# Retention streamed in 128-token tiles of all heads, transposes by DMA, and a different split of ELU over the engines

## The chip, the cores and the metric

The kernel runs on one core of one Trainium2 chip. The metric is the device time of one execution in microseconds (us). Most executions of one kernel agree within about 1%. A run counts as slow when it is over 1.5% above the fastest run of the same kernel. Ratios use the others, the fast runs: a ratio is the mean time of one kernel's fast runs over the mean time of the other's fast runs of the same rounds, so it is not quite the ratio of the medians that are quoted. In brackets stands its 95% interval. Under 1, the new kernel is faster.

Names used below: PE is TensorE (matrix products), ACT is ScalarE, DVE is VectorE, POOL is GpSimd, SP is SyncE (here it only starts DMAs). In these kernels PE writes its products to tiles in PSUM; all other tiles lie in SBUF. FFN is the feed-forward part, FFN1 its first product and FFN2 its second.

## The reference

```python
# B, H, S, D = 8, 8, 576, 64; all inputs and the output are float32
scores = (1 / sqrt(D)) * q @ k.T                    # per batch and head
gamma  = 1 - 2.0 ** (-5 - arange(H))
ret    = scores * (gamma ** (i - j) if i >= j else 0)   # decay, causal, no softmax
x      = (ret @ v)  -> transposed to tokens x (H*D) = (4608, 512)
h      = x @ w_in                                   # 512 x 2048
g      = where(h > 0, h, exp(min(h, 0)) - 1)        # ELU
out    = g @ w_out                                  # 2048 x 512
```

Because the decay is a product of a factor for row i and one for row j, both kernels multiply q and k by it once and only mask the scores. It also means that everything before a block of tokens can be folded into a D x D state per head: `state = sum over earlier tokens of k_j v_j^T`.

Both kernels compute ELU as `min(max(h, 0), exp(h) - 1)`: `exp` on ACT, then a subtraction of 1, then one max/min instruction on DVE. This identity holds as `exp(h) - 1 >= h`.

## The kernel before

It treats one batch at a time. For each pair of heads it forms the lower triangle of the scores over 576 tokens in four 128-blocks and a tail of 64; only between the first 256 tokens and the rest does it use a state. A generator yields pieces of that work, which the program deals out between the FFN pieces; the order on PE is the scheduler's.

```python
    def attn(b, loads):
        ...                                     # (cut: tails)
        def prep(hp):                           # one head pair, 512 tokens
            ...
            nc.vector.tensor_tensor(qn, r["q"]..., gq..., ALU.mult)
            nc.gpsimd.tensor_tensor(kn, r["k"]..., gk..., ALU.mult)
            nc.scalar.copy(vn.transpose([0, 2, 1, 3]), r["v"])
            return qn, kn, vn

        def trans(hp, qn, kn):                  # q, k turned on PE, copied out by ACT
            ...
            for i, n in enumerate((qn, kn)):
                for t in range(2):
                    nc.tensor.transpose(p0[:, i, t * P : (t + 1) * P], n[:, t], ident)
            nc.scalar.copy(qkT[:, :, :C0], p0)
            ...                                 # (cut: the other two blocks and the tail)

        def scores(qkT, blocks, mask):
            n = mask.shape[1]
            sc = [ps_s.tile([P, n], FP32, name="sc", tag="sc") for _ in range(2)]
            for kt, lo, hi in blocks:
                for i in range(2):              # the two heads of the pair
                    r = slice(i * D, (i + 1) * D)
                    nc.tensor.matmul(sc[i][:, o : o + hi - lo],
                        qkT[r, 1, kt * P : (kt + 1) * P], qkT[r, 0, lo:hi], ...)
                ...
            for i in range(2):
                nc.vector.tensor_tensor(p, sc[i], mask, ALU.mult)
        ...
        for hp in range(HP):
            ...
            pa = scores(qkT, ((0, 0, C0), (1, P, C0), (4, FT * P, S)), mask0)
            yield
            pb = scores(qkT, ((2, C0, S), (3, C0 + P, S)), mask1)
            ...                                 # (cut: products with v and the state)

    def ffn1(g, ft):                            # 128 of 2048 columns, 512 tokens
        xt = xt_tile(g)
        ph = ps_h.tile([P, TG], FP32, name="ph", tag="ph")      # 3 buffers
        for j in range(KJ):
            nc.tensor.matmul(ph, w_in_sb[:, j, ft * P : (ft + 1) * P], xt[:, j], ...)
        e = epool.tile([P, TG], FP32, name="e", tag="e")
        nc.scalar.activation(e, ph, AF.Exp)
        nc.gpsimd.tensor_scalar_add(e, e, -1.0)
        gt_ = gpool.tile([P, TG], BF16, name="g", tag="g")
        nc.vector.scalar_tensor_tensor(gt_, ph, 0.0, e, ALU.max, ALU.min)

    for g in range(NTG + 1):                    # 9 groups of 512 tokens
        ...                                     # (cut: loads two batches ahead)
        for s in range(NFT):
            if g < NTG: ffn1(g, s)
            if g > 0:   ffn2(g - 1, s)
            for _ in range(2 if s % 2 == 0 else 1):
                next(steps, None)               # a piece of batch g + 1
```

Of the kernel before, what the change touches and what calls it, by code (L numbers as in the profile page):

```python
# [17 lines left out]
def kernel(  # L18
# [17 lines left out]
    C0 = 256  # L36
    C1 = S - C0
    FT = 4
    ST = S - FT * P
    KJ = DM // P  # L40
# [4 lines left out]
    assert (DM, S, D, ST) == (H * D, 576, 64, 64)  # L45

    const = ctx.enter_context(tc.tile_pool(name="const", bufs=1))
    raw = ctx.enter_context(tc.tile_pool(name="raw", bufs=5))
    nat = ctx.enter_context(tc.tile_pool(name="nat", bufs=4))
    tpool = ctx.enter_context(tc.tile_pool(name="tpool", bufs=3))  # L50
    ppool = ctx.enter_context(tc.tile_pool(name="ppool", bufs=4))
    wst = ctx.enter_context(tc.tile_pool(name="wst", bufs=6))
    xpool = ctx.enter_context(tc.tile_pool(name="xpool", bufs=3))
    gpool = ctx.enter_context(tc.tile_pool(name="gpool", bufs=2 * NFT + 2))
    epool = ctx.enter_context(tc.tile_pool(name="epool", bufs=5))
# [4 lines left out]
    ps_t = ctx.enter_context(tc.tile_pool(name="ps_t", bufs=1, space=PSUM))  # L60
    ps_s = ctx.enter_context(tc.tile_pool(name="ps_s", bufs=2, space=PSUM))
    ps_o = ctx.enter_context(tc.tile_pool(name="ps_o", bufs=1, space=PSUM))


    ident = const.tile([P, P], BF16, name="ident")
    make_identity(nc, ident)

# [3 lines left out]
    for h in range(H):  # L71
        nc.vector.memset(lgt[:, h : h + 1], lg[h])
    pos_i = const.tile([P, FT + 1], I32, name="pos_i")
# [3 lines left out]
    pos = const.tile([P, FT + 1], FP32, name="pos")  # L77
# [8 lines left out]
    expo = const.tile([P, FT + 1, H], FP32, name="expo")  # L86
    nc.vector.tensor_tensor(
        expo,
        pos.unsqueeze(2).to_broadcast([P, FT + 1, H]),
        lgt.unsqueeze(1).to_broadcast([P, FT + 1, H]),  # L90
        ALU.mult,
    )
    gq = const.tile([P, FT, H], FP32, name="gq")
    nc.scalar.activation(gq, expo[:, :FT], AF.Exp, bias=bq)
    gk = const.tile([P, FT, H], FP32, name="gk")
    nc.scalar.activation(gk, expo[:, :FT], AF.Exp, bias=bk, scale=-1.0)
    gt = const.tile([P, H], FP32, name="gt")
    nc.scalar.activation(gt, expo[:, FT], AF.Exp, bias=bt)


    mask0 = const.tile([P, 448], BF16, name="mask0")
    mask1 = const.tile([P, 512], BF16, name="mask1")
    nc.vector.memset(mask0, 1.0)
    nc.vector.memset(mask1, 1.0)
    for m, lo, n in ((mask0, 0, 256), (mask0, 256, 128), (mask0, 384, 64), (mask1, 0, 320), (mask1, 320, 192)):
        nc.gpsimd.affine_select(
            out=m[:, lo : lo + n], in_=m[:, lo : lo + n], compare_op=ALU.is_ge, fill=0.0,
            base=0, pattern=[[1, n]], channel_multiplier=-1,
        )


    sbd = []
    for i in range(2):
        s = const.tile([P, HP, P], BF16, name=f"sbd{i}")
        nc.gpsimd.memset(s, 0.0)
        sbd.append(s)

# [4 lines left out]
    def w_in_piece(n, cast):  # L122
        w = 512
        for j in range(KJ):
            t = wst.tile([P, 512], FP32, name="wst", tag="wst")
            nc.scalar.dma_start(t, moe_w_in[j * P : (j + 1) * P, n * w : (n + 1) * w])
            cast[j % len(cast)](w_in_sb[:, j, n * w : (n + 1) * w], t)  # L127

    def w_out_piece(f, cast):
        t = wst.tile([P, 512], FP32, name="wst", tag="wst")  # L130
        nc.scalar.dma_start(t, moe_w_out[f * P : (f + 1) * P, :])
        cast(w_out_sb[:, f, :], t)


    def load_pair(b, hp):
        r = {}
        h0 = 2 * hp
        for nm, src in (("q", q), ("k", k), ("v", v)):
            t = raw.tile([P, 2, FT, D], FP32, name="r" + nm, tag="r" + nm)
            for i in range(2):  # L140
                nc.sync.dma_start(
                    t[:, i], src[b, h0 + i, : FT * P, :].rearrange("(t p) d -> p t d", p=P)
                )
            r[nm] = t
        return r

    def load_tails(b):
        rt = raw.tile([P, H, D], FP32, name="rt", tag="rt", bufs=2)
        nc.sync.dma_start(rt[:ST], q[b, :, FT * P :, :].rearrange("h p d -> p h d"))
        nc.sync.dma_start(rt[ST:], k[b, :, FT * P :, :].rearrange("h p d -> p h d"))  # L150
        rv = raw.tile([ST, H, D], FP32, name="rv", tag="rvt", bufs=2)
        nc.sync.dma_start(rv, v[b, :, FT * P :, :].rearrange("h p d -> p h d"))
        return rt, rv

    xts = {}
# [6 lines left out]
    def put_x(b, hp, lo, n, src):  # L162
        t0 = b * S + lo
        while n:
            g, o = divmod(t0, TG)
            m = min(n, TG - o)
            nc.scalar.copy(xt_tile(g)[:, hp, o : o + m], src[:, :m])  # L167
            src = src[:, m:]
            t0 += m
            n -= m  # L170

    def attn(b, loads):
        rt, rv = loads["t"]
        qkt = nat.tile([P, H, D], BF16, name="qkt", tag="qkt", bufs=2)
        nc.vector.tensor_tensor(qkt, rt, gt.unsqueeze(2).to_broadcast([P, H, D]), ALU.mult)
        vt = nat.tile([P, H, D], BF16, name="vt", tag="vt", bufs=2)
        nc.gpsimd.memset(vt[ST:], 0.0)
        nc.gpsimd.tensor_copy(vt[:ST], rv)
        yield
        sb = sbd[b % 2]  # L180

        def prep(hp):
            h0 = 2 * hp
            r = loads[hp]
            qn = nat.tile([P, FT, 2, D], BF16, name="qn", tag="qn")
            nc.vector.tensor_tensor(  # L186
                qn, r["q"].transpose([0, 2, 1, 3]),
                gq[:, :, h0 : h0 + 2].unsqueeze(3).to_broadcast([P, FT, 2, D]), ALU.mult,
            )
            kn = nat.tile([P, FT, 2, D], BF16, name="kn", tag="kn")  # L190
            nc.gpsimd.tensor_tensor(  # L191
                kn, r["k"].transpose([0, 2, 1, 3]),
                gk[:, :, h0 : h0 + 2].unsqueeze(3).to_broadcast([P, FT, 2, D]), ALU.mult,
            )
            vn = nat.tile([P, FT, 2, D], BF16, name="vn", tag="vn")
            nc.scalar.copy(vn.transpose([0, 2, 1, 3]), r["v"])  # L196
            return qn, kn, vn

        def trans(hp, qn, kn):
            h0 = 2 * hp  # L200
            qkT = tpool.tile([P, 2, S + 64], BF16, name="qkT", tag="qkT")
            nc.gpsimd.memset(qkT[:, 1, S:], 0.0)  # L202
            p0 = ps_t.tile([P, 2, C0], BF16, name="p0", tag="tr")
            for i, n in enumerate((qn, kn)):
                for t in range(2):
                    nc.tensor.transpose(p0[:, i, t * P : (t + 1) * P], n[:, t], ident)  # L206
            nc.scalar.copy(qkT[:, :, :C0], p0)
            yield qkT
            p1 = ps_t.tile([P, 2, C1], BF16, name="p1", tag="tr")
            for i, n in enumerate((qn, kn)):  # L210
                for t in range(2):
                    nc.tensor.transpose(p1[:, i, t * P : (t + 1) * P], n[:, 2 + t], ident)
            nc.tensor.transpose(p1[:, :, 2 * P :], qkt[:, h0 : h0 + 2], ident)
            nc.scalar.copy(qkT[:, :, C0:S], p1)
            yield qkT

        def state(hp, kn, vn):
            st = ps_o.tile([P, P], FP32, name="st", tag="o")
            for t in range(2):
                nc.tensor.matmul(st, kn[:, t], vn[:, t], start=(t == 0), stop=(t == 1))  # L220
            nc.vector.tensor_copy(sb[:D, hp, :D], st[:D, :D])
            nc.vector.tensor_copy(sb[D:, hp, D:], st[D:, D:])

        def scores(qkT, blocks, mask):
            n = mask.shape[1]
            sc = [ps_s.tile([P, n], FP32, name="sc", tag="sc") for _ in range(2)]
            o = 0
            for kt, lo, hi in blocks:
                for i in range(2):
                    r = slice(i * D, (i + 1) * D)  # L230
                    nc.tensor.matmul(  # L231
                        sc[i][:, o : o + hi - lo], qkT[r, 1, kt * P : (kt + 1) * P], qkT[r, 0, lo:hi],
                        start=True, stop=True,
                    )
                o += hi - lo
            pt = []
            for i in range(2):
                p = ppool.tile([P, n], BF16, name="pt", tag=f"pt{n}")
                nc.vector.tensor_tensor(p, sc[i], mask, ALU.mult)  # L239
                pt.append(p)  # L240
            return pt

        def av0(hp, vn, pa):
            o = ps_o.tile([P, C0], FP32, name="o0", tag="o")
            for kt, lo, c in ((0, 0, 0), (1, P, C0)):
# [7 lines left out]
        def av1(hp, vn, qkT, pa, pb):  # L253
# [3 lines left out]
            for kt, lo, src, c in ((2, 0, pb, 0), (3, P, pb, C1), (4, 2 * P, pa, 384)):  # L257
                for i in range(2):
# [4 lines left out]
                    )  # L263
            put_x(b, hp, C0, C1, o)

        nxt = prep(0)
        yield
        for hp in range(HP):
            qn, kn, vn = nxt
# [108 lines left out]
```

## Time and profile before

The median of the first three runs was 432.2 us (431.96 to 432.32).

| Quantity | Before | Where it is read |
|---|---|---|
| span of the profiled run | 429.6 us | page, first line |
| PE busy | 367.1 us (85%) | page, part 1 |
| POOL busy, of it for the -1 of ELU | 264.5, 215.2 us | page, parts 1 and 5 |
| first FFN1 product starts | 40.6 us | timeline of PE |
| one group of 512 tokens with one batch of retention | 42.6 us | timeline of PE, 143.5 to 313.9 |

The first fence holds lines of the page of the kernel before. Part 1 gives each engine's busy time. The row PE is the busy share in tenths of 40 equal slices. Part 4 is the chain of work that ended last, by engine and by line. Each line of part 5 is a group of instructions: line, engine, operation, output and inputs, count, then the busy time and the mean in ns, then the idle time of the engine before them and what ended it.

```profile
PE 367.1 (85%) x2176; PEld 162.5 (38%) x2176; DVE 226.6 (53%) x408; ACT 197.2 (46%) x388; POOL 264.5 (62%) x240
PE   0017959998999998999999999999999999999975
...
PE 48%; POOL 18%; DMA 11%; DVE 9%; issue 7%; ACT 6%; SPq 1%; POOLq 0%; ACTq 0%; DVEq 0%
...
L295 POOL TENSOR_SCALAR e<-e 128x512 f32<-128x512 f32 x144 | 215.2, 1498 | 84.7 <-ACT e L294 82.8
L297 DVE SCALAR_TENSOR_TENSOR g<-ph,e 128x512 bf16<-128x512 f32 x144 | 99.4, 691 | 136.3 <-POOL e L295 136.2
```

PE is nearly always busy from 45 us on, yet the chain that ended last goes through POOL for 18% of the span. The -1 of one 128x512 tile takes POOL 1498 ns, against 599 for the `exp` on ACT, and DVE stood 136.2 us in all waiting for it.

The next fence is the timeline of PE in the kernel before: start, time, what, number of matmuls, and in brackets the idle time before it.

```profile
228.83 1.03 PE L290 MATMUL ph<-xt,w_in_sb 128*128 128x512 bf16 x4
229.70 1.03 PE L308 MATMUL pm<-w_out_sb,g 128*128 128x512 bf16 x4
230.56 0.28 PE L212 MATMUL p_2782<-ident,qn 128*128 128x128 bf16 x2
...
232.46 1.03 PE L308 MATMUL pm<-w_out_sb,g 128*128 128x512 bf16 x4
233.87 0.38 PE L231 MATMUL sc<-qkT 64*128 64x320 bf16 x2 [0.38 <-DVE pt L239]
234.17 0.39 PE L290 MATMUL ph<-xt,w_in_sb 128*128 128x512 bf16 x1
234.50 0.39 PE L231 MATMUL sc<-qkT 64*128 64x320 bf16 x2
```

Starts matter here, as the time given for a matmul is longer than the distance to the next start (0.39 against 0.216 us for one of the FFN). Four FFN matmuls are followed by the next after 0.865 us, 216 ns each, so the 128 of a group take 27.7 us. The rest of the 42.6 us, 15 us, is one batch of retention and its waits. The two score products of one head start at 233.87 and are followed 0.30 us later: 320 and 192 columns of one head took about as long as 512 columns of the FFN (216 ns) and a switch (the lone FFN matmul at 234.17 is followed after 0.33 us, 0.11 more than the 216 ns), so no second head ran beside them. None of the score products of 320 and 192 columns begins beside that of the other head; of those of 256, 128 and 64 columns most do (54, 54 and 56 of 64 begin within 8 ns of their partner), so the kernel before has part of this pairing already. The scores also wait for DVE to free their PSUM buffer, 17.3 us in all.

### The profile page before, as it was taken

How to read it: one execution, taken by the hardware profiler on the slowest of the kernel's cores; microseconds unless marked ns; L12 is line 12 of the kernel's file. 1: busy time of each engine (PE TensorE's matmuls, PEld its weight loads, DVE VectorE, ACT ScalarE, POOL GpSimd, SP SyncE). 2: the span in 40 equal slices, each digit the busy share in tenths (PEclk: the TensorE clock that was granted, in tenths of full speed). 3: DMA queues.
4: the chain of work that ended last, by engine and by line, in shares of the span. 5: the costliest groups of instructions: out<-in, count | busy, mean ns of one | idle time of the engine just before them, and what ended most of it. 6: DMA issues, size and time to landing. Idle time of an engine off the chain costs nothing.

```text
span 429.6 us, 6300 instructions
## 1 busy us (share of the span) xinstructions
PE 367.1 (85%) x2176; PEld 162.5 (38%) x2176; DVE 226.6 (53%) x408; ACT 197.2 (46%) x388; POOL 264.5 (62%) x240
## 2 busy tenths in 40 slices
PE   0017959998999998999999999999999999999975
PEld 0003414433444444443444444444444444444432
DVE  2326547767655665657566656665555544433310
ACT  2244446663445444545454455455544444434411
POOL 3311239887666776686667666766565558888810
PEclk9999999998999999999999999999999999999999
DMA  8999789809416837655555331100010001101011
GB/s 220 288 260 286 194 223 223 155 0 196 97 29 147 185 96 175 147 139 132 137 122 136 85 89 49 51 24 2 24 50 25 2 25 50 44 31 49 24 58 65
DMA packets 123871, 46.55 MB, mean 108 GB/s; under 512 B 115136, under 2 KB 115136, under 8 KB 123840
## 3 DMA queue, kind: packets, MB, share of 16 engines
q1 hardware_dynamic: 119232, 37.76, 37.4%
q10 hardware_dynamic: 4608, 8.39, 6.3%
q8 instruction: 17, 0.28, 0.3%
q14 instruction: 14, 0.11, 0.1%
HBM read 36.70 MB, written 9.44 MB: 107 GB/s over the span
## 4 chain that ended last, share of the span: by engine, by line
PE 48%; POOL 18%; DMA 11%; DVE 9%; issue 7%; ACT 6%; SPq 1%; POOLq 0%; ACTq 0%; DVEq 0%
PE ph L290 19%; POOL e L295 17%; PE pm L308 15%; PE sc L231 5%; DVE pt L239 5%; ACT e L294 3%; DMA rq<-in_q_dram 2%; DMA wst<-in_moe_w_in_dram 2%; DMA rv<-in_v_dram 2%; DMA wst<-in_moe_w_out_dram 2%; DVE g L297 1%; DMA rk<-in_k_dram 1%; ACT xt L167 1%; ACT ot L313 1%; DMA rt<-in_k_dram 1%
## 5 line engine op out<-in xcount | busy, mean ns | idle before, releaser
L295 POOL TENSOR_SCALAR e<-e 128x512 f32<-128x512 f32 x144 | 215.2, 1498 | 84.7 <-ACT e L294 82.8
L297 DVE SCALAR_TENSOR_TENSOR g<-ph,e 128x512 bf16<-128x512 f32 x144 | 99.4, 691 | 136.3 <-POOL e L295 136.2
L290 PE MATMUL ph<-xt,w_in_sb 128*128 128x512 bf16 x576 | 162.5, 389 | 2.0 <-DVE g L297 1.4
L308 PE MATMUL pm<-w_out_sb,g 128*128 128x512 bf16 x576 | 149.5, 381 | 3.0 <-ACT ot L313 2.9
L294 ACT ACTIVATE e<-ph 128x512 f32<-128x512 f32 x144 | 86.3, 599 | 102.7 <-PE ph L290 100.9
L308 PEld LDWEIGHTS <-g 128*128 128x128 bf16 x576 | 55.5, 98 | 69.1 <-issue 7.9
L290 PEld LDWEIGHTS <-w_in_sb 128*128 128x128 bf16 x576 | 48.9, 99 | 53.6 <-issue 11.2
L231 PE MATMUL sc<-qkT 64*128 64x320 bf16 (+4 forms) x320 | 43.1, 261 | 18.8 <-DVE pt L239 17.3
L191 POOL TENSOR_TENSOR kn<-rk,gk 128x512 bf16<-128x512 f32 x32 | 33.8, 1056 | 24.2 <-DMA rk<-in_k_dram 18.0
L239 DVE TENSOR_TENSOR pt<-sc,mask_136 128x512 bf16<-128x512 f32 x64 | 41.7, 684 | 1.2 <-PE sc L231 1.0
L239 DVE TENSOR_TENSOR pt<-sc,mask_135 128x448 bf16<-128x448 f32 x64 | 37.2, 619 | 6.3 <-PE sc L231 5.6
L231 PEld LDWEIGHTS <-qkT 64*128 64x128 bf16 x320 | 17.1, 96 | 51.6 <-issue 46.4
L313 ACT COPY ot<-pm 128x512 f32<-128x512 f32 x36 | 21.2, 588 | 31.2 <-PE pm L308 31.2
L186 DVE TENSOR_TENSOR qn<-rq,gq 128x512 bf16<-128x512 f32 x32 | 26.9, 846 | 10.8 <-DMA rq<-in_q_dram 1.9
L196 ACT CAST vn<-rv 128x512 bf16<-128x512 f32 x32 | 19.8, 620 | 12.4 <-PE o_1345 L260 0.9
L202 POOL MEMSET qkT<- 128x64 bf16 x32 | 4.8, 153 | 31.0 <-PE o_370 L256 6.2
L220 PE MATMUL st<-vn,kn 128*128 128x128 bf16 x64 | 9.6, 232 | 16.2 <-ACT vn L196 16.2
L220 PEld LDWEIGHTS <-kn 128*128 128x128 bf16 x64 | 6.4, 105 | 22.6 <-issue 17.7
L127 DVE CAST w_in_sb<-wst 128x512 bf16<-128x512 f32 x8 | 3.9, 486 | 16.5 <-DMA wst<-in_moe_w_in_dram 16.5
L206 PEld LDWEIGHTS <-qn 128*128 128x128 bf16 x64 | 5.1, 100 | 17.5 <-DVE qn L186 12.4
L260 PEld LDWEIGHTS <-vn 128*64 128x64 bf16 x128 | 5.8, 111 | 15.4 <-issue 15.3
L127 ACT CAST w_in_sb<-wst 128x512 bf16<-128x512 f32 x8 | 4.9, 618 | 14.2 <-DMA wst<-in_moe_w_in_dram 14.2
(459 smaller groups left out, 242.2 us busy)
## 6 DMA issues: line engine op xcount, KB each, us to landing
rv<-in_v_dram SPq DMA_DIRECT2D x72, 128.0 KB, 3.2
out_dram<-ot SPq DMA_DIRECT2D x36, 256.0 KB, 2.1
rq<-in_q_dram SPq DMA_DIRECT2D x64, 128.0 KB, 3.2
rk<-in_k_dram SPq DMA_DIRECT2D x64, 128.0 KB, 3.1
wst<-in_moe_w_in_dram ACTq DMA_DIRECT2D x16, 256.0 KB, 5.0
wst<-in_moe_w_out_dram ACTq DMA_DIRECT2D x16, 256.0 KB, 3.6
rt<-in_q_dram SPq DMA_DIRECT2D x8, 128.0 KB, 3.7
rt<-in_k_dram SPq DMA_DIRECT2D x8, 128.0 KB, 4.1
```

The lines of the kernel that those rows point to most:

```text
L186: nc.vector.tensor_tensor(qn, r["q"].transpose([0, 2, 1, 3]), gq[:, :, h0 : h0 + 2].unsqueeze(3).to_broadcast([P, FT, 2, D]), ALU.mult,)
L191: nc.gpsimd.tensor_tensor(kn, r["k"].transpose([0, 2, 1, 3]), gk[:, :, h0 : h0 + 2].unsqueeze(3).to_broadcast([P, FT, 2, D]), ALU.mult,)
L196: nc.scalar.copy(vn.transpose([0, 2, 1, 3]), r["v"])
L220: nc.tensor.matmul(st, kn[:, t], vn[:, t], start=(t == 0), stop=(t == 1))
L231: nc.tensor.matmul(sc[i][:, o : o + hi - lo], qkT[r, 1, kt * P : (kt + 1) * P], qkT[r, 0, lo:hi], start=True, stop=True,)
L239: nc.vector.tensor_tensor(p, sc[i], mask, ALU.mult)
L290: nc.tensor.matmul(ph, w_in_sb[:, j, ft * P : (ft + 1) * P], xt[:, j], start=(j == 0), stop=(j == KJ - 1))
L294: nc.scalar.activation(e, ph, AF.Exp)
L295: nc.gpsimd.tensor_scalar_add(e, e, -1.0)
L297: nc.vector.scalar_tensor_tensor(gt_, ph, 0.0, e, ALU.max, ALU.min)
L308: nc.tensor.matmul(pm, gts[g, ft][:, it * P : (it + 1) * P], w_out_sb[:, ft], start=(ft == 0), stop=(ft == NFT - 1))
L313: nc.scalar.copy(ot, pm)
```

## The change

Its intent is to take work from PE and latency from ELU:

- Retention goes by 128-token tiles of all eight heads (four and a tail of 64 per batch, 40 in all). Only the diagonal block of the scores is formed; all earlier tokens come in through the state, which PE sums in PSUM from tile to tile and ACT copies to SBUF.
- q and k are turned by the DMA engines (the first four tiles still on PE); their multiply with the decay is one POOL instruction of 128x1024; v is cast to bf16 by its own load, started by POOL.
- The -1 of ELU moves from POOL, in place in float32, to DVE, from float32 to bf16.
- FFN1 of the first group starts after four tiles instead of a batch, and the order on PE is pinned to that of the program.

```diff
+    def mm(*a, **kw):
+        tc.keep_in_program_order(nc.tensor.matmul(*a, **kw))
...
+    def load(s):                       # s counts tiles, 5 per batch
+        ...
+        for dst, src in parts:
+            dma = nc.gpsimd.dma_start if src is v else nc.sync.dma_start
+            dma(dst, src[b, :, rows, :].rearrange("h p d -> p h d"))
+    def cast(s):
+        ...
+                nc.gpsimd.tensor_tensor(qkn, rqk, g, ALU.mult)
+    def turn(s):
+        ...
+        if s < FT:
+            for i in range(2):         # on PE, copied out by DVE and ACT
+                ...
+        else:
+            nc.sync.dma_start_transpose(qkT, flat)
+    def scores(s):
+        ...
+        for hp in range(HP):
+            for i in range(2):
+                r = slice(i * D, (i + 1) * D)
+                mm(sc[:, i, hp * n : (hp + 1) * n], kT[r, hp], qkT[r, hp, :n], start=True, stop=True)
+        nc.vector.tensor_tensor(pt, sc, mask, ALU.mult)       # (views cut)
+    def state(s):
+        ...
+                mm(st[i * D : (i + 1) * D, hp], qkn[:, 1, h], vn[:, h],
+                   start=(t == 0 and hp == 0), stop=True, skip_group_check=True)
+        sb = sbd[s % 2]
+        nc.scalar.copy(sb[:D, :, :D], st[:D])
+        nc.scalar.copy(sb[D:, :, D:], st[D:])
...
     def ffn1(g, ft):
         nc.scalar.activation(e, ph, AF.Exp)
-        nc.gpsimd.tensor_scalar_add(e, e, -1.0)
+        em = epool.tile([P, TG], BF16, name="em", tag="em")
+        nc.vector.tensor_scalar_add(em, e, -1.0)
-        nc.vector.scalar_tensor_tensor(gt_, ph, 0.0, e, ALU.max, ALU.min)
+        nc.vector.scalar_tensor_tensor(gt_, ph, 0.0, em, ALU.max, ALU.min)
...
+    # start: tiles 0-3 first, then
+    for f in range(NFT):
+        w_out_piece(f)                 # 16 loads in SP's queue
+    for s in range(FT + 2, FT + AHEAD_L):
+        load(s)
+    for s in range(FT, FT + AHEAD_C):
+        cast(s)
+    for s in range(FT, FT + AHEAD_T):
+        turn(s)                        # DMA transposes, same queue
+    run([[a] for a in f1(0)], FT)                    # FFN1(0), tile 4 inside it
+    run([[a] for a in f2(0)], last_step(1) + 1)      # FFN2(0), tiles 5-9
+    run([[a] for a in f1(1)], last_step(2) + 1)      # FFN1(1), tiles 10-13
+    for g in range(2, NTG):                          # FFN1(g) beside FFN2(g - 1)
+        ...
```

## The prediction

> **What bounds it now.** TensorE. By slices it is 90-99% busy from 45 us on; the first feed-forward (FFN) matmul starts at 40.6 us (timeline). After that one batch of retention rides on each FFN token group, and a group takes 42.6 us (four stretches, 143.5 to 313.9). FFN matmuls follow each other every 216 ns (four in 0.865 us), so a group's 128 cost 27.7 us; retention and its stalls take 15. The timeline gives retention about 2.5 us per head pair, 10.1 per batch, most of it scores (300-320 ns for 320+192 columns, the two heads not issued side by side), transposes, value products and shape switches. The rest is waiting: scores on the DVE mask multiply 17.3 us in all (waits), and the FFN chain exp 0.60, POOL -1 1.50, DVE 0.69. The POOL -1 is 17% of the chain that ended last.
>
> **What changes.** Removed: 256 of 288 PE transposes, their ACT copies, most of the lower triangle (only diagonal 128-blocks remain), ACT casts of v, the POOL -1 (215 us, 1.5 of latency per tile). Added: 36 DMA transposes of up to 256 KB, a DVE -1 (f32 to bf16, SBUF; a weight cast of that shape takes 0.43), two small ACT state copies per tile, POOL multiplies of 128x1024 (twice 1.05). The instruction order shows head pairs side by side, and FFN1(0) after four tiles, not a batch.
>
> **Cost after, estimates from these durations.** FFN 1152 x 216 ns = 249 us. Retention per 128-token tile: 28 small matmuls at 27-56 ns plus switches, about 1.5 us (a tail 1.0): 56 us in all against 81. Per group about 34.5 us, of which DVE has 18 (-1, min/max) + 5.5 (masks), ACT about 18.
>
> The PE saving is all on the critical path, but three things eat into it:
> 1. Start: FFN1(0) at about 23 us, then held by w_in (landed about 30 us) and, near its end, by the tail tile, whose DMA transpose stands behind all of w_out and three loads in one queue: FFN1(0) ends about 53 us.
> 2. FFN2(0) and FFN1(1) run unpaired: about 22 and 25 us, the second bound by DVE (1.12 per tile, PE 0.86).
> 3. POOL holds DVE: [...] The trace agrees: a weight cast takes 0.43 alone, 0.69 when begun 0.41 before a POOL multiply ends. A 2.1 us multiply can thus delay the new -1; three h buffers hide most. About 1 us per group.
>
> Paired groups 2 to 8: 7 x 27.7 + 38 + 8 = 240 us. Tail as now 20 us.
>
> Sum: 53 + 22 + 25 + 240 + 20 = **360 us**, 8 in 10 between 335 and 395. Faster by over 2%: 0.90; within 2%: 0.03; slower: 0.07.
>
> **Right if:** the -1 leaves POOL and the chain; a paired group takes 33-36 us; retention's PE time falls to about 55 us; PE waits cluster before 100 us, released by transposes or w_out; DVE's -1 is about 0.45 us, some near 2.
>
> **Wrong if:** the DMA transposes are slow; no trace here has one. [...] Also if DVE saturates (POOL holding it), or pinned PE order exposes waits that the old scheduler filled. Faster than 335 if the start stalls little.

## The result, and the profile after

The median fell from 432.08 us (431.01 to 432.32) to 353.61 us (352.11 to 356.05), four runs each. The ratio is 0.8193 [0.8144, 0.8242]. A later repeat of the changed kernel as it is (the control of the experiments), with five rounds, gave 351.6 us, 0.8148 [0.811, 0.8185].

The fence holds the lines of the page of the kernel after that answer to those shown of before, with the row of PE's granted clock in tenths of full speed.

```profile
PE 303.9 (86%) x2208; PEld 149.2 (42%) x2208; DVE 233.2 (66%) x371; ACT 162.5 (46%) x312; POOL 104.8 (30%) x93
PE   1278720999868999999999999999999999999985
PEclk9999975799998999999999999999999999999999
...
PE 74%; DVE 8%; DMA 8%; SPq 4%; ACT 3%; issue 1%; POOL 0%; ACTq 0%; POOLq 0%
...
L301 DVE TENSOR_SCALAR em<-e 128x512 bf16<-128x512 f32 x144 | 83.5, 581 | 56.5 <-ACT e L299 56.3
L303 DVE SCALAR_TENSOR_TENSOR g<-ph,em 128x512 bf16<-128x512 f32 x144 | 99.2, 691 | 5.5
```

The -1 is gone from POOL and POOL from the chain (18% to 0%), which is now PE for 74% of the span. Where the time came from is read from the starts of FFN1 of each group in the two timelines of PE:

| Stretch | Before, us | After, us | Saved, us |
|---|---|---|---|
| start to FFN1 of group 2 | 139.0 | 112.0 | 27.0 |
| FFN1 of group 2 to FFN1 of group 8 | 241.6 | 193.7 | 47.9 |
| FFN1 of group 8 to the end | 49.0 | 48.6 | 0.4 |
| sum (the profiled spans) | 429.6 | 354.3 | 75.3 |

The starts of FFN1 of groups 2 and 8 in the timeline of PE in the kernel before:

```profile
139.00 1.03 PE L290 MATMUL ph<-xt,w_in_sb 128*128 128x512 bf16 x4
...
380.63 1.03 PE L290 MATMUL ph<-xt,w_in_sb 128*128 128x512 bf16 x4
```

And of groups 3 and 8 in the timeline of PE in the kernel after (that of group 2, at 112.04, is inside a merged line):

```profile
146.30 1.03 PE L65 MATMUL ph<-xt,w_in_sb 128*128 128x512 bf16 x4
...
305.70 1.03 PE L65 MATMUL ph<-xt,w_in_sb 128*128 128x512 bf16 x4
```

The largest part comes from the steady groups: 31.9 us each from FFN1 of group 3 at 146.3 to that of group 8 at 305.7, instead of 42.6. The timeline of PE in the kernel after shows one full tile of retention inside such a group.

```profile
181.23 0.39 PE L65 MATMUL o<-qkT,sbd_144 128*128 128x128 bf16 x4
181.55 0.40 PE L65 MATMUL sc<-qkT 64*128 64x128 bf16 x8
181.88 0.41 PE L65 MATMUL o<-pt,vn 128*64 128x128 bf16 x8
182.12 0.29 PE L65 MATMUL st<-vn,qkn 128*64 128x64 bf16 x8
182.35 0.60 PE L65 MATMUL ph<-xt,w_in_sb 128*128 128x512 bf16 x2
```

From 181.23 to 182.35, 28 matmuls take 1.12 us, with no wait. The eight score products (the second line) take 0.33 us, 41 ns each, while the four full-height products of the same 128 columns above them take 0.32 us, 80 ns each. So in this trace two heads of 64 rows go side by side in the time of one; within each pair the second begins 3 to 4 ns after the first. Not every tile costs 1.12 us: the first of a batch takes 0.91, the second 0.80 (as the tile before it has no product with a state) and the tail 0.89, so a batch costs PE about 0.91 + 0.80 + 2 x 1.12 + 0.89 = 4.8 us. The groups say the same: 31.9 - 27.7 = 4.2 us for 512 of a batch's 576 tokens.

The next fence is the table of busy time by stretch: first 146.3 to 308.1, then 50 to 64 us, in the kernel after. Its columns are the stretch, its length, busy time and count of PE, PEld, DVE, ACT and POOL, then granted clock, DMA share, GB/s.

```profile
146.30:308.10 161.80, 161.80 (x1197) 79.53 (x1196) 122.78 (x187) 82.67 (x158) 37.00 (x28) 1.00 0.57 103
50.00:64.00 14.00, 2.10 (x13) 0.92 (x14) 1.54 (x3) 1.85 (x3) 5.71 (x3) 0.50 0.96 219
```

In the steady part, of which this window reaches 2.4 us into group 8, PE has no gap at all, 161.80 of 161.80 us. The hole is at the start. The following lines are the timeline of SP's queue in the kernel after; what it starts is counted there as long as it takes to issue.

```profile
32.14 16.28 SPq L141 DMA_DIRECT2D wst<-in_moe_w_out_dram  x16
...
58.37 1.50 SPq L203 DMA_TRANSPOSE qkT<-qkt  x1
```

And the timeline of PE in the kernel after, at the same time:

```profile
45.90 1.02 PE L65 MATMUL ph<-xt,w_in_sb 128*128 128x512 bf16 x4 [0.25 <-DVE g L303]
61.90 0.39 PE L65 MATMUL sc<-qkT 64*128 64x64 bf16 x8 [14.97 <-DMA qkT<-qkt]
62.22 3.60 PE L65 MATMUL ph<-xt,w_in_sb 128*128 128x512 bf16 x8
```

PE stands 14.97 us for the transpose of the first tail, which is issued at 58.37 us, behind the 16 loads of w_out and three more tiles' loads. Afterwards eight FFN matmuls take 3.60 us where eight at 216 ns take 1.7. The granted clock was 0.50 from 50 to 64 us. It was down to 0.50 by 49.0 us, when PE had stood for about 2 us.

### The profile page after: what moved, and what is told of

The parts are those of the page before. It is cut to its first block, busy times and chain, and to the rows that moved or that the text cites. A ratio compares the mean times of both kernels' runs of the same rounds, so it can differ in the third digit from the quotient of the medians.

```text
span 354.3 us, 5834 instructions
## 1 busy us (share of the span) xinstructions
PE 303.9 (86%) x2208; PEld 149.2 (42%) x2208; DVE 233.2 (66%) x371; ACT 162.5 (46%) x312; POOL 104.8 (30%) x93
## 3 DMA queue, kind: packets, MB, share of 16 engines
q0 software_dynamic: 37504, 4.72, 20.8%
HBM read 36.70 MB, written 9.44 MB: 130 GB/s over the span
## 4 chain that ended last, share of the span: by engine, by line
PE 74%; DVE 8%; DMA 8%; SPq 4%; ACT 3%; issue 1%; POOL 0%; ACTq 0%; POOLq 0%
PE pm L65 35%; PE ph L65 30%; PE o L65 5%; DVE em L301 4%; DVE g L303 3%; PE sc L65 3%; SPq L164 3%; DMA wst<-in_moe_w_out_dram 2%; DMA rqk<-in_k_dram 2%; DMA wst<-in_moe_w_in_dram 2%; DVE pt L217 1%; SPq L136 1%; ACT ot L315 1%; DMA qkT<-qkt 1%; ACT e L299 1%
## 5 line engine op out<-in xcount | busy, mean ns | idle before, releaser
L65 PE MATMUL ph<-xt,w_in_sb 128*128 128x512 bf16 x576 | 150.0, 388 | 10.8 <-DVE g L303 9.7
L301 DVE TENSOR_SCALAR em<-e 128x512 bf16<-128x512 f32 x144 | 83.5, 581 | 56.5 <-ACT e L299 56.3
L303 DVE SCALAR_TENSOR_TENSOR g<-ph,em 128x512 bf16<-128x512 f32 x144 | 99.2, 691 | 5.5
L179 POOL TENSOR_TENSOR qkn<-rqk,gtab 128x1024 bf16<-128x1024 f32 x28 | 53.4, 1907 | 46.1 <-DMA rqk<-in_k_dram 26.8
L164 POOL DMA_DIRECT2D vn<-in_v_dram x32 | 29.8, 935 | 57.2 <-PE st L65 37.3
L217 DVE TENSOR_TENSOR pt<-sc,mask 128x1024 bf16<-128x1024 f32 x32 | 38.9, 1216 | 7.8 <-PE sc L65 7.8
L254 ACT CAST xt<-o 128x512 bf16<-128x512 f32 (+1 forms) x44 | 22.0, 509 | 38.4 <-PE o L65 37.9
L65 PE MATMUL sc<-qkT 64*128 64x128 bf16 (+1 forms) x320 | 16.2, 225 | 23.4 <-DMA qkT<-qkt 15.0
L65 PEld LDWEIGHTS <-qkT 64*128 64x128 bf16 x320 | 9.4, 99 | 30.4 <-DMA qkT<-qkt 15.5
L65 PE MATMUL o<-pt,vn 128*64 128x128 bf16 x256 | 14.4, 239 | 0.0
L65 PE MATMUL st<-vn,qkn 128*64 128x64 bf16 x256 | 10.0, 203 | 0.0
```

The source lines that it names most:

```text
L65: tc.keep_in_program_order(nc.tensor.matmul(*a, **kw))
L164: dma(dst, src[b, :, rows, :].rearrange("h p d -> p h d"))
L179: nc.gpsimd.tensor_tensor(qkn, rqk, g, ALU.mult)
L217: nc.vector.tensor_tensor(pt.rearrange("p i h n -> p (i h) n") if n == P else pt, sc.rearrange("p i (h n) -> p (i h) n", h=HP) if n == P e ...
L254: nc.scalar.copy(xt_tile(g)[:, :, off : off + w], o[:, :, c : c + w])
L301: nc.vector.tensor_scalar_add(em, e, -1.0)
```

## The experiments

Three questions were open: how the 78 us divide over the parts of the change; whether the hole at the start can be closed, and what makes it; and whether POOL's hold on DVE costs anything. On the hole there were two main theories. One (the queue; theory Q below) says that the tail's transpose stands at a bad place in SP's queue. The other (the traffic; theory or rival D below) says that what the first groups need arrives no earlier, in whatever order it is asked for. "Time in the rings" is the time that the profile counts for the packets of the 16 DMA engines; as a share of these engines' time it is the DMA share, which can pass 1 (1.43 from 30 to 50 us in the kernel after). All 12 runs gave correct results. They ran in three sets, each on one chip with its own runs of the kernel before (432.25, 432.27 and 432.32 us). Only the second set has the changed kernel itself in it, so in the others the ratios to the kernel before carry the comparison.

### The -1 back on POOL, in the kernel after

```diff
-        em = epool.tile([P, TG], BF16, name="em", tag="em")
-        nc.vector.tensor_scalar_add(em, e, -1.0)
+        nc.gpsimd.tensor_scalar_add(e, e, -1.0)
+        em = e
```

> The changed kernel with one thing undone: the -1 of the ELU back on POOL, in place in f32. My theory (TensorE's own work for retention is what fell; the ELU move matters because POOL now also has the 1.9 us multiplies of q and k): POOL gets 144 x 1.5 = 216 us on top of its 105, about 320 us of busy time, close to saturated beside the paired groups, so h buffers are held longer and PE waits for DVE g rise well above 9.7 us; 375 us (range 362 to 395). Rival A (the move of the -1 is the main gain of the change): 410 us or more. Rival B (the -1 was never on the path): within 2% of 354.

Measured: 382.86 us (381.79 to 383.36), ratio 0.8857 [0.8833, 0.8881]. As expected. Two lines of the waits of this kernel (who waited for whom: us in all, times, longest):

```profile
DVE g L303 <- POOL e L300: 171.4, 140, 6.2
...
PE ph L65 <- DVE g L303: 29.9, 29, 2.8
```

And its busy time by stretch, with the columns as above:

```profile
150.00:200.00 50.00, 46.41 (x334) 22.46 (x333) 21.46 (x28) 23.31 (x46) 49.84 (x36) 0.97 0.95 162
```

POOL was busy for 49.84 of these 50 us. With the -1, the multiplies of 128x1024 and the starts of v's loads, POOL became the limit, and PE waited for g 29.9 us instead of 9.7. So in the changed kernel the move of the -1 is worth 29 us. By the starts of FFN1 in the two profiles (27 us apart in all), 19 us come before group 3 (165.4 us against 146.3) and 8 between group 3 and group 8, where a group takes 33.5 us instead of 31.9.

### The -1 to DVE alone, in the kernel before

```diff
-        nc.gpsimd.tensor_scalar_add(e, e, -1.0)
+        em = epool.tile([P, TG], BF16, name="em", tag="em")
+        nc.vector.tensor_scalar_add(em, e, -1.0)
-        nc.vector.scalar_tensor_tensor(gt_, ph, 0.0, e, ALU.max, ALU.min)
+        nc.vector.scalar_tensor_tensor(gt_, ph, 0.0, em, ALU.max, ALU.min)
```

> The kernel before with one part of the change alone: the -1 on DVE, written as bf16. My theory: the paired groups are bound by TensorE (40 of 42.6 us busy), so at most the 2 to 3 us of PE waits per group and the slower start of the first group can come back: 420 us (range 410 to 430), group period about 41. Rival A (the ELU chain is the main gain, because its POOL op is 17% of the chain): below 395.

Measured: 413.24 us (413.1 to 414.09), ratio 0.9568 [0.9546, 0.9589]. This falls within the expectation, and the rival (that the move alone brings most of the gain) falls. A stretch slightly longer than one steady group (FFN1 starts at 174.55 and 215.09, 40.5 us apart), in the table of busy time by stretch of this kernel:

```profile
174.80:215.70 40.90, 40.76 (x259) 18.18 (x258) 31.78 (x63) 21.88 (x42) 7.05 (x11) 1.00 0.58 139
```

Now PE is busy for 40.76 of 40.90 us: the ELU chain's latency explained about 2 us per group (42.6 to 40.5), and the remaining 12.8 us above 27.7 are retention's work on PE. The rewrite brings them to about 4.8 per batch. Eight batches at 8.0 us are 64 us, an estimate from these numbers; measured between this kernel and the change are 413.24 - 353.61 = 59.6 us. By the starts of FFN1, 35.2 us of the difference of the profiled spans (57.1) come between group 2 and group 8, the paired groups that the estimate is about, and 21.7 before group 2, where PE also waits.

Together with the first experiment: the move alone gave 19.0 us, all the rest alone 49.4 us, both 78.6 us (against 432.25). So 10 us come only from having both: the faster PE needs the ELU chain faster than POOL can do it.

### The transposes back on PE

```diff
-        if s < FT:
-            for i in range(2):
+        if s < FT or s >= FT + 2:
+            for i in range(n // HP):
```

> The changed kernel with q and k of all tiles but the tail tile 4 and tile 5 turned by PE transposes and copied out by DVE and ACT, as its first four tiles are. My theory: 27 full tiles cost PE 8 x 56 ns plus a switch, about 0.5 us, the tails 0.27: 15 us more PE time, all on the path, plus some waits for the h buffers that the transposes share: 371 us (range 364 to 385). Rival (the DMA transposes cost as much as they save, because they load the DMA rings and their queue): within 2% of 354, or faster.

Measured: 370.47 us (369.33 to 371.51), ratio 0.8568 [0.8537, 0.8599]. As expected. The 244 transposes cost 17 to 19 us (against 353.61 and 351.6), 69 to 77 ns each on PE. The copies out of PSUM cost PE nothing more in the steady part: it is still busy 150.00 of 150 us from 150 to 300. Tiles 4 and 5 kept their DMA transposes, so this does not touch the hole, which was 15.3 us here.

### The order on PE not pinned

```diff
     def mm(*a, **kw):
-        tc.keep_in_program_order(nc.tensor.matmul(*a, **kw))
+        nc.tensor.matmul(*a, **kw)
```

The same was done to the PE transposes. It ran twice, the second time with five rounds on another chip.

> The changed kernel without the pinned order of the matmuls; the scheduler places them. My theory: the paired groups have no PE gap that order could close, so only the pairing of the two heads' small matmuls can be lost: if the scheduler splits pairs as in the kernel before, each tile pays up to 0.3 us, 10 us in all: 354 to 365. Rival C (the pinned order is a main part of the gain): 375 or more.

> The changed kernel without the pinned order again, as a control and to tell a 1% difference: 350 us against 351 to 354 with it, all of it before 110 us; the paired groups have the same period.

Measured: 350.13 us (348.85 to 352.73), ratio 0.8111 [0.8069, 0.8152]; again 350.17 us (349.4 to 351.21), ratio 0.8098 [0.8076, 0.812]. The pinned order gains nothing; without it the kernel is about 1% faster, below the 2% that would count, and the intervals of the ratios with and without it just overlap. The first expectation (354 to 365) was missed: the scheduler did not split the pairs, and the paired groups have the same period (31.9 us from FFN1 of group 3 at 141.45 to that of group 8 at 300.86 in the repeat). Timeline of PE in the unpinned kernel:

```profile
42.34 0.38 PE L65 MATMUL pm<-w_out_sb,g 128*128 128x512 bf16 x1 [0.99 <-DVE w_out_sb L142]
...
55.45 5.99 PE L65 MATMUL pm<-w_out_sb,g 128*128 128x512 bf16 x16 [0.67 <-ACT ot L313]
...
65.66 0.29 PE L65 MATMUL sc<-qkT 64*128 64x64 bf16 x8
```

Here FFN2 of group 0 starts at 42.3 us and fills the time before the tail's transpose; the tail's scores come at 65.66 us without a wait. From 40 to 64 us PE was busy 18.4 us, against 6.6 in the kernel after. Yet only 1.5 to 3.5 us stay in the end (medians of 350.13 and 350.17 us against 351.6 and 353.61): the retention of tiles 5 to 9 then stood from 66 to 79 us with few FFN matmuls left to fill its waits (one of 2.17 us for POOL's multiply).

### The tail's transpose earlier in the queue

```diff
+    cast(FT)
     for f in range(NFT):
         w_out_piece(f)
+        if f == 7:
+            turn(FT)
+            cast(FT + 1)
+        if f == 11:
+            turn(FT + 1)
```

The later `cast` and `turn` of these tiles are dropped. The unchanged kernel ran beside it as a control.

> The changed kernel with the DMA transposes of the tail tile 4 and of tile 5 issued in the middle of the w_out loads, not after them and three more tile loads. Theory Q (the 15 us wait is queue order): the wait goes, PE finishes the first layer of group 0 about 12 us earlier; w_out itself is all cast by 53.5 us and tile 6 only arrives at 57, so part comes back as waits for those: 345 us (342 to 349). Rival D (the start is bound by bytes: the DMA rings are full until about 100 us, and any order moves the wait elsewhere): 352 or more.

> The changed kernel as it is, as a control beside the next three on the same chip: 353 to 354 us, PE waiting about 15 us for the DMA transpose of the first tail tile, and 10 us for DVE in the unpaired first layer of group 1.

Measured: 353.01 us (350.92 to 354.94), ratio 0.8163 [0.8125, 0.82], against 351.6 us (350.71 to 355.05), 0.8148, of the control. The expectation was missed: nothing gained. The control itself came out 1.4 us below what was expected of it, with a wait of 12.9 us for the transpose and 3.8 for DVE in FFN1 of group 1. Timeline of PE in the kernel with the early transposes:

```profile
47.88 0.29 PE L65 MATMUL sc<-qkT 64*128 64x64 bf16 x8 [1.49 <-DMA qkT<-qkt]
...
56.34 0.38 PE L65 MATMUL pm<-w_out_sb,g 128*128 128x512 bf16 x1 [0.81 <-DVE w_out_sb L142]
...
67.54 0.61 PE L65 MATMUL sc<-qkT 64*128 64x128 bf16 x8 [5.77 <-DMA qkT<-qkn]
```

The wait for the tail did shrink, from 12.9 us in the control to 1.5, and FFN1 of group 0 ended at 51.5 us instead of 64.0. But FFN2 of group 0 ended at 84.7 us, in the control at 84.6. In between PE waited four times for pieces of w_out, then 5.77 us for the transpose of tile 6, whose multiply on POOL began only at 60.9 us after a wait for its load of k. PE then ran at half clock (granted 0.50 from 62 to 68 us). The wait was moved, not removed: the queue place explains where PE stood, not when the stage ended. By the landings in the traces, what was not moved came later: the last piece of w_out at 58.0 us (53.3 in the control), the k of tile 6 at 60.7 (55.3). The q of tile 6 was issued at nearly the same time, 49.5 and 49.2 us, and landed at 59.5 instead of 54.2. So that delay arose after the issue, not while SP held it back, which speaks for the traffic (the two transposes were now ahead of it).

### Two tiles of v fewer loaded ahead

```diff
-... nat.tile([P, H, D], BF16, name="vn", tag="vn", bufs=8)
+... nat.tile([P, H, D], BF16, name="vn", tag="vn", bufs=6)
```

> The changed kernel with 6 v buffers for 8: one number. The first 30 us then carry v of 6 full tiles, not of 8 or more, before w_in and w_out. Rival D (bytes bind the start): w_in and w_out land 2 to 4 us earlier and so does everything after: 350 to 352. Theory Q (queue order alone): within 1 us of the control.

Measured: 353.81 us (349.46 to 355.01), ratio 0.8158 [0.8115, 0.8201]. Not distinguishable from the control, so the gain that one theory expected did not show. Its own sign did not show either: the last pieces of w_in and w_out landed at 31.9 and 53.2 us, in the control at 31.5 and 53.3, where 2 to 4 us earlier was expected. It takes only two tiles out of the first 30 us, too little to tell the theories apart. One of the six runs was slow and is not in the ratio.

### v loaded by SP in float32, cast by ACT

```diff
-            dma = nc.gpsimd.dma_start if src is v else nc.sync.dma_start
-            dma(dst, ...)
+            nc.sync.dma_start(dst, ...)        # v into a float32 tile rv
...
     def cast(s):
+        nc.scalar.copy(vn[vp], rv[vp])
```

> The changed kernel with v loaded as f32 by the SP queue like q and k and cast by ACT, in place of the casting DMA of POOL. Theory D (the DMA rings bind the start; the casting queue took 20.8% of 16 engines' span for v, about 74 us, where the kernel before spent by estimate 40 us on the same v as f32): the first 60 us carry about 10 us less ring time, the wait for the first tail tile falls from 13-15 us to 8 or less, group 1's first layer ends near 100 us, not 108-113: 340 to 346 us. Rival (something else than ring time paces the arrivals, or the ACT casts cost as much): 350 or more.

The 40 us in it are estimated from the page of the kernel before: queue q1 took 37.4% of 429.6 us for 37.76 MB, of which v is 9.44.

Measured: 357.38 us (356.85 to 359.0), ratio 0.8272 [0.8248, 0.8295]: slower than the change, where 340 to 346 was expected. The theory behind it was that the casting loads of v hold the DMA rings and delay the others. Its busy time by stretch:

```profile
0.00:30.00 30.00, 17.16 (x156) 10.77 (x157) 14.63 (x40) 15.28 (x32) 7.52 (x17) 1.00 1.01 232
30.00:50.00 20.00, 10.05 (x40) 3.74 (x39) 17.80 (x33) 11.62 (x21) 2.95 (x2) 0.97 0.86 215
50.00:65.00 15.00, 0.00 (x0) 0.00 (x0) 1.28 (x3) 3.71 (x6) 3.80 (x2) 0.50 1.12 256
```

In the first 30 us the DMA share fell from 1.29 (the change) to 1.01, so transfers did spend less time in the rings, and a piece of w_in landed in a median of 4.6 us instead of 6.8. Part of the fall is that only 4 loads of v were issued in these 30 us, instead of 14. Still the rate was 232 GB/s in both. In the three stretches the change moved 232, 259 and 217 GB/s, so 15.4 MB by 65 us; this kernel 15.1 MB. So less time in the rings brought no higher rate in bytes as counted; a casting load counts half of what it reads (the page of the kernel after has 4.72 MB for v, which is 9.44 MB in float32), so this alone does not rule the rings out. Whether it matters which engine starts a load, no run here tests alone. Over the whole run the time in the rings of all queues of loads, stores and transposes was 71.8% of 16 engines' span of 357.3 us, against 79.6% of 354.3 us in the kernel after (20.8 of the 79.6 for the casting loads of v): some 25 us less. The edit did gain something: FFN1 of group 0 began at 23.8 us instead of 28.7. The loss has a visible cause: the v loads now stand in SP's queue too, the tail's transpose was issued at 62.55 instead of 58.37 us, and PE waited 22.5 us. So the run changes two things at once, and it does not settle the theory.

An estimate for the traffic theory: the weights (8.4 MB) and q, k, v of tiles 0 to 8 (6.7 MB) make 15.1 MB, at about 235 GB/s (the two kernels' mean rates to 65 us were 237 and 232) 64 us. The last of these loads, the k of tile 8, landed at 61.3 us in the kernel after and at 65.3 in the early-transpose kernel. The estimate is consistent with both runs, but not proven by itself: loads of later tiles of v are among the traffic, v's bytes count half where the load casts them, and the rate varied by stretch.

### The multiply on POOL in two halves

```diff
-                nc.gpsimd.tensor_tensor(qkn, rqk, g, ALU.mult)
+                nc.gpsimd.tensor_tensor(qkn[:, 0], rqk[:, 0], g[:, 0], ALU.mult)
+                nc.gpsimd.tensor_tensor(qkn[:, 1], rqk[:, 1], g[:, 1], ALU.mult)
```

The prediction said that POOL holds DVE, so that a multiply can delay the -1. The timeline of DVE in the kernel after shows it:

```profile
92.70 0.42 DVE L301 TENSOR_SCALAR em<-e 128x512 bf16<-128x512 f32 x1
...
94.23 2.14 DVE L301 TENSOR_SCALAR em<-e 128x512 bf16<-128x512 f32 x1
```

And the timeline of POOL in the same kernel:

```profile
94.19 1.90 POOL L179 TENSOR_TENSOR qkn<-rqk,gtab 128x1024 bf16<-128x1024 f32 x1 [3.19 <-DMA rqk<-in_k_dram]
```

A -1 alone takes 0.42 us; the one begun beside the multiply took 2.14, and ended at 96.37, 0.28 us after the multiply. The halves were to cap this. A clause of the expectation is cut, as no run shows the mechanism that it names; its first numbers hold on condition that the multiply is what holds the -1.

> The changed kernel with each 1.9 us multiply of POOL split into two of about 1.05 us. [...] the longest -1 falls from over 2.2 us to about 1.4 and its mean from 0.58 to about 0.53; the PE waits for DVE g, 10 us before, fall by 2 to 4 us, the total by no more than that: 348 to 352. If the -1 is slow for another reason, its durations stay as they are.

Measured: 354.11 us (351.36 to 357.34), ratio of the fast runs 0.8165 [0.8136, 0.8195]: no gain. The profiled run was a slow one (its total is not used), but what overlaps what is still readable. Timeline of DVE in this kernel:

```profile
102.04 2.42 DVE L302 TENSOR_SCALAR em<-e 128x512 bf16<-128x512 f32 x1
```

And the timeline of POOL in this kernel:

```profile
102.12 1.06 POOL L179 TENSOR_TENSOR qkn<-rqk,gtab 128x512 bf16<-128x512 f32 x1
103.12 1.04 POOL L180 TENSOR_TENSOR qkn<-rqk,gtab 128x512 bf16<-128x512 f32 x1
```

The -1 was held through both halves, 2.42 us. The longest was 2.68 us, where about 1.4 was expected, and the mean 604 ns, against 581. The expectation was missed. A hold that ended with the first half would have let DVE in at 103.2. Here the halves, which follow each other at once, held as one: the second begins at 103.12, before the first ends. By its record the -1 begins at 102.04, 0.08 us before the first half, and is held all the same, so here the order of the recorded starts does not tell which of the two is held. The unchanged kernel had shown this already: its longest -1, 2.54 us from 112.10, ran beside a multiply of 128x1024 from 111.44 and one of 128x512 from 113.31, again without a pause. Whether a pause between them would let DVE in was not tried.

### Half of the -1 of FFN1 of group 1 on ACT

```diff
+        if g == 1 and ft % 2:
+            nc.scalar.activation(em, e, AF.Copy, bias=-1.0)
+        else:
             nc.vector.tensor_scalar_add(em, e, -1.0)
```

> The changed kernel with the -1 of every second tile of the unpaired first layer of group 1 on ACT. If that stretch (86 to 113 us) is bound by DVE, as its 90% busy time and the 10 us of PE waits for DVE g say: half or more of these waits go, 347 to 350 us. If it is bound by the arrival of tiles: within 1 us of the control.

Measured: 351.5 us (350.47 to 355.61), ratio 0.8152 [0.8111, 0.8193], the same as the control within its spread, where 347 to 350 was expected. In the trace, PE's waits for g in FFN1 of group 1 fell from 3.8 to 2.1 us, and the stage from the end of FFN2 of group 0 to the end of FFN1 of group 1 took 20.7 us instead of 23.1, so that stage is partly bound by DVE, but this run's hole at the start was 2.6 us longer (15.5 against 12.9). The effect is smaller than the noise of the start, and the total is inconclusive.

### Unpinned, v by SP, and half the -1 on ACT together

This combines three of the edits shown above.

> Three edits together on the changed kernel: no pinned order, v by the SP queue with ACT casts, the -1 of half of group 1's first layer on ACT. If the start is bound by ring time and then by DVE, and PE can fill waits when order is free: 333 to 341 us, with group 1's first layer done by 95. If not: 346 or more.

Measured: 355.96 us (355.2 to 356.36), ratio 0.8236 [0.8213, 0.8258]. Missed: it is worse than the unpinned kernel alone (350.17). The loss of v by SP, measured alone in the same set, is as large as this difference (357.38 against the control's 351.6), so the half of the -1 on ACT shows no gain here. The best version found is the unpinned one.

## Why the prediction was right, and where it was off

The predicted 360 us stands against 353.61, in the range, and the mechanism held: PE bounds the kernel and the time falls by what leaves PE's path. Point by point:

- **The -1 leaves POOL and the chain:** right. POOL's share of the chain fell from 18% to 0%. The two experiments on it size it at 19 us alone and 29 us in the changed kernel.
- **A paired group takes 33 to 36 us:** just below, 31.9. The term was mis-sized: retention takes at most 1.12 us per full tile, not 1.5, and a batch 4.8, not 7.0. That is 39 us of PE time in all, where about 55 was named as a sign of being right. Of the 8 us of stalls that were added 1.5 came, all in group 2. The stretch put at 240 us took about 220, from FFN1 of group 2 at 112.0 to the end of FFN1 of group 8 at 332.6.
- **The start, FFN1 of group 0 ending at about 53 us:** this step was wrong in size, 65.8 us. It began at 28.7 us, not at 23. The place of the longest wait was named rightly, the tail's transpose behind w_out and three loads in one queue, but the wait was taken as short; it was 14.97 us, and half clock followed (granted 0.50 from 50 to 64 us). An experiment shows that moving it up alone brings nothing: other data of the same stage then landed some 5 us later.
- **FFN2 of group 0 and FFN1 of group 1, 22 and 25 us:** 20.7 and 25.7. That DVE binds part of the second is supported by PE's waits for g, 5.3 of their 9.7 us lie there, and by the experiment's shorter stage; its total was inconclusive.
- **POOL holds DVE, about 1 us per group:** the hold is real, with a median of 0.43 us and a longest of 2.5 for the -1, as said. In the steady groups it cost PE nothing, as PE has no gap there. That the three buffers of h hid it, as predicted, was not tested.
- **DMA transposes slow?** No: a median of 4.0 us from issue to landing for the full tiles (list of DMA issues), 3.0 to 7.5 over all 36, and 1.2 us or more of SP's queue each. They save 17 to 19 us against PE transposes.
- **Pinned order exposes waits that the scheduler filled:** named as a risk, and true to about 1%: the scheduler fills the hole at the start with FFN2, but gives most of it back.

So the two misses partly cancelled: FFN1 of group 0 ended 13 us later than predicted, the paired groups took 20 us less (the other three terms were off by under 2 us each). That the total came within 2% is in part luck; it did not mean that each term was as close.

What stays open: whether the arrival of data in the first 65 us is limited by the memory, by the DMA engines or by how the loads are shaped; and how the 43 us of the rewrite beyond the DMA transposes (59.6 - 17) divide over the diagonal-only scores, the two heads side by side and the earlier start.

## What to carry to other kernels

When PE is nearly saturated, cost a change by the matmul time that it removes from each steady group, and check with an experiment whether a slower engine's chain was a second limit close behind: here POOL would have taken back 29 us of the gain. Before moving one late transfer forward, add up everything that the same stage must load: here the sum of bytes filled the time by estimate, and the wait only moved to the next tile. And read the terms of a good prediction singly, as errors of opposite sign hide in the sum.
